# One gated recurrence and a two-branch layer on one core: block 0's layers taken by quarters of the weights, and the input casts and transposing DMAs run as a pipeline of single tensors, three items ahead

## The chip, the core and the metric

The kernel runs on one core of a Trainium2 chip. Its engines work side by side, each through its own queue in program order, and they wait for one another by semaphores: TensorE (PE in the profile; its weight loads are listed as PEld), VectorE (DVE), ScalarE (ACT), GpSimd (POOL) and SyncE (SP), which here only issues DMAs. Sixteen DMA engines serve all DMA queues of the core. The metric is the device time of one execution in microseconds. Time before: 400.93 us, the median of 6 runs (400.65 to 401.17).

## The reference

The input `x` and `f_logit` are 4 x 6144 x 256 in fp32, `lower_bound` has 256 entries. The first part is a recurrence over time, one for each batch row and channel; the second is a layer with two branches, of which the larger is kept:

```python
sig = 1 / (1 + exp(-f_logit))
f = lower_bound + (1 - lower_bound) * sig
for t in range(S):                       # S = 6144
    h = f[:, t] * h + (1 - f[:, t]) * x[:, t]
    y[:, t] = h
h1 = y @ w1;  h2 = y @ w2                # 256 -> 1024
out = max(h1, h2) @ w_out                # 1024 -> 256
```

## The kernel before, in words

**The algebra.** With u = sigmoid(-f_logit) and om = 1 - lower_bound, 1 - f is om * u. The kernel scans y' = ff * y' + u * x with ff = 1 - om * u, so that the true y is om * y'; the factor om is put into the weights. max(h1, h2) is h1 + relu(h2 - h1), so it makes `wd` = om * (w2 - w1) in bf16, and `w13` = om * (w1 @ w_out), which needs w1 transposed (`w1T`). The output is relu(y' @ wd) @ w_out + y' @ w13.

**The tiles.** Time is cut into 48 blocks of 512 steps (`TB`), 12 for each batch row. Channels lie on the partitions, in two halves (`KC` = 2). For a block, `hidden(j, fc)` makes one of eight chunks of 128 hidden units: two matmuls of 512 columns into a PSUM tile `dT`, then a relu into `rt` (ScalarE, or VectorE where `on_dve`). `project_steps(j, i, lo, hi)` makes a quarter i of the block's tokens out of eight `rt` chunks and two steps with `w13`: ten matmuls of 256 columns into `psO`. A block thus has 16 hidden and 40 projecting matmuls. `store` copies a PSUM tile to SBUF and issues the DMA to the output from SP.

**The input.** The natural layout has time on the rows, so it must be transposed. Blocks 0 to 2 are loaded in fp32 (`load`), turned to u and v in natural layout (`gate_nat`, `drive_nat`), and transposed by TensorE (`turn_pe`); then come `forget` (ff) and `scan`. From block 3 on, POOL issues DMAs that copy `f_logit` and `x` to DRAM scratch with a cast to bf16 (`cast`, tiles `fs` and `xs`), and SP issues transposing DMAs from there into SBUF (`turn_dma`, tiles `fT` and `xT`); `gate`, `drive`, `forget` and `scan` then work in the transposed layout. Before, an item of this chain is a chunk of two blocks (`CB` = 2; the first has one), both tensors together, with two sets of scratch (`NS`). POOL holds the next cast back by a one-column copy (`held`) out of the transposed tile before it (`cast_after_turn`).

**The order.** Everything runs under `tc.manual_schedule()`: the program order below is each engine's order. Loads first (L397 to L416): they alternate blocks of `x`, `f_logit` and quarters of w1 and w2, and w_out in two halves. Then block 0 and the making of the weights are woven together by hand (L421 to L517): `diff` (w2 - w1) on POOL, the last quarter on VectorE; `scale` (times om) on ScalarE; `turn_w1` transposes w1 in fp32 on TensorE, `keep_w1` copies it out; `linear_weights` makes w13's sums in two halves. `keep_warm` issues matmuls on zeros. The main loop (L525) does for block j and chunk fc: hidden(j, fc), a half-slot of projection of block j - 1, and, at places given by the tables `gate_at` and `turn_of` (L378 to L384), the gate and scan of a block two ahead and the transposing DMAs of a chunk three ahead. Block 1's projection is done in the loop pass j = 2.

Of the kernel before, what the change touches and what calls it, by code (L numbers as in the profile page):

```python
# [12 lines left out]
P = 128  # L13
# [3 lines left out]
def kernel(  # L17
# [25 lines left out]
    NP = 3  # L43
    CB = 2
    assert NBB % CB == 0
    chunks = [(NP, 1)] + [(j, CB) for j in range(NP + 1, NBLK, CB)]
    NCH = len(chunks)
    home = {j + o: (c, o) for c, (j, n) in enumerate(chunks) for o in range(n)}
    NS = 2
# [8 lines left out]
    ttpool = ctx.enter_context(tc.tile_pool(name="turned", bufs=3))  # L58
# [3 lines left out]
    opool = ctx.enter_context(tc.tile_pool(name="opool", bufs=4))  # L62
# [11 lines left out]
    w1n = wpool.tile([P, KC, DFF], FP32)  # L74
    w2n = wpool.tile([P, KC, DFF], FP32)
# [63 lines left out]
    def scan(j, h, t0=0, t1=TB):  # L139
# [18 lines left out]
    rows, chunk = {}, {}  # L158

    spare = {  # L160
        (k, name): scratch.tile([CB * TB, D], BF16, name=f"{name}{k}")
# [4 lines left out]
    def cast(c):  # L166
        j, n = chunks[c]
        b, k = divmod(j, NBB)
        rows[c] = []
        for name, src in (("fs", f_logit), ("xs", x)):  # L170
            t = spare[c % NS, name]
            nc.gpsimd.dma_start(  # L172
                out=t[0 : n * TB, :],
                in_=src[b, k * TB : (k + n) * TB, :],
                max_dma_last_dim=4096,
            )
            rows[c].append(t)

    def turn_dma(c):
        n = chunks[c][1] * TB  # L180
        for s in range(2):
            t = ttpool.tile([P, KC, CB * TB], BF16, name=("fT", "xT")[s])
            chunk[c, s] = t
            nc.sync.dma_start_transpose(out=t[:, :, 0:n], in_=rows[c][s][0:n, :])

    def gate(j):
        c, o = home[j]
        us[j] = midpool.tile([P, KC, TB], BF16, name="u")
        nc.scalar.activation(  # L189
            out=us[j][:],  # L190
            in_=chunk[c, 0][:, :, o * TB : (o + 1) * TB],
            func=AF.Sigmoid,
            scale=-1.0,
        )
        uT[j] = us[j]

    def drive(j):
        c, o = home[j]
        vT[j] = midpool.tile([P, KC, TB], BF16, name="v")
        nc.vector.tensor_tensor(  # L200
            out=vT[j][:],
            in0=us[j][:],
            in1=chunk[c, 1][:, :, o * TB : (o + 1) * TB],
            op=ALU.mult,
        )
# [67 lines left out]
    def store(j, g):  # L273
        osb = opool.tile([P, 2, D], FP32, name="osb")
        nc.vector.tensor_copy(out=osb[:], in_=pos[j, g, 0][:])  # L275
        r0 = j * TB + 2 * g * P
        nc.sync.dma_start(
            out=out[r0 : r0 + 2 * P, :].rearrange("(p r) d -> p r d", r=2), in_=osb[:]
        )

    def store_row(j, g, r):
        osb = opool.tile([P, 2, D], FP32, name="osb")
        ps = pos[j, g, r]
        nc.vector.tensor_copy(out=osb[:, 0, 0:P], in_=ps[:, 0, 0:P])
        nc.scalar.copy(out=osb[:, 0, P:D], in_=ps[:, 0, P:D])
# [3 lines left out]
            in_=osb[:, 0, :],  # L289
# [5 lines left out]
    def weight_load(k, w, src):  # L295
        cols = slice(k * QF, (k + 1) * QF)
# [4 lines left out]
    def wout_load(g):  # L301
        nc.sync.dma_start(
            out=won[:, 4 * g : 4 * g + 4, :],
            in_=moe_w_out[g * HF : (g + 1) * HF, :].rearrange("(q p) c -> p q c", p=P),
# [20 lines left out]
    def scale(k, h):  # L325
        cols = slice(k * QF, (k + 1) * QF)
        nc.scalar.activation(
            out=wd[:, h, cols], in_=wdf[:, h, cols], func=AF.Copy, scale=om[:, h : h + 1]
        )

    pts = {}

    def turn_w1(k):
        pts[k] = ps_d.tile([P, 2, D], FP32, name="dT")
        for q in range(2):
            for h in range(KC):
                nc.tensor.transpose(
                    pts[k][:, q, h * P : (h + 1) * P],
                    w1n[:, h, unit(2 * k + q)],
                    ident[:],  # L340
                )

    def keep_w1(k):
        nc.scalar.copy(out=w1T[:, 2 * k : 2 * k + 2, :], in_=pts[k][:])
# [33 lines left out]
    gate_at = {NP: (1, 7), NP + 1: (3, 2), NP + 2: (3, 6), NP + 3: (5, 0), NP + 4: (5, 5)}  # L378
    gate_at |= {b: (b - 2, 5) for b in range(NP + 5, NBLK)}
    gate_of = {}  # L380
    for b, at in gate_at.items():
        gate_of.setdefault(at, []).append(b)
    turn_of = {(1, 3): 1}
    turn_of |= {(chunks[c][0] - 3, 5): c for c in range(2, NCH)}  # L384

    def cast_after_turn(c):

        last = chunks[c - 1][1] * TB - 1
        nc.gpsimd.tensor_copy(out=held[:], in_=chunk[c - 1, 0][:, KC - 1, last : last + 1])  # L389
        cast(c)  # L390

    with tc.manual_schedule():
# [4 lines left out]
        nc.scalar.dma_start(out=lbr[:], in_=lower_bound.rearrange("(h p) -> h p", p=P))  # L397
        load(0, 0, 0, 2)
        load(0, 1, 0, 2, nc.scalar)
        for k in range(2):  # L400
            weight_load(k, w1n, moe_w1)
            weight_load(k, w2n, moe_w2)
            if k == 0:
                load(0, 0, 2, 4)
                load(0, 1, 2, 4)
        wout_load(0)
        for k in range(2, 4):
            weight_load(k, w1n, moe_w1)
            weight_load(k, w2n, moe_w2)
        for s in range(2):  # L410
            load(1, s, 0, 2)
        wout_load(1)
# [8 lines left out]
        keep_warm(6)  # L421
        keeps()
        keep_warm(2)


        gate_nat(0, 0, 2)
        drive_nat(0, 0, 2)
        for s in range(2):
            for q in range(2):
                turn_pe(0, s, q)  # L430
        forget(0, 0, 0, HB, on_act=True)
        forget(0, 1, 0, HB)
        for h in range(KC):
            scan(0, h, 0, HB)
        diff(0, 0, KC, nc.gpsimd)
        turn_w1(0)
        keep_warm(3)
        gate_nat(0, 2, 4)
        drive_nat(0, 2, 4)
        for s in range(2):  # L440
            for q in range(2, 4):
                turn_pe(0, s, q)
        scale(0, 0)
        forget(0, 0, HB, TB, on_act=True)
        forget(0, 1, HB, TB)
        scale(0, 1)
        keep_w1(0)
        for fc in range(2):
            hidden_cols(0, fc, 0, HB)
        for h in range(KC):  # L450
            diff(1, h, h + 1, nc.gpsimd)
        for h in range(KC):
            scan(0, h, HB, TB)
        turn_w1(1)
        for h in range(KC):
            scale(1, h)
        nc.gpsimd.tensor_copy(out=wob[:, 0:4, :], in_=won[:, 0:4, :])
        for fc in range(2):
            hidden_cols(0, fc, HB, TB)
            relu(0, fc, on_dve=(fc == 1))  # L460
        for fc in range(2, 4):
            hidden(0, fc, on_dve=(fc == 3))
        keep_w1(1)
        for h in range(KC):
            diff(2, h, h + 1, nc.gpsimd)
        for h in range(KC):
            scale(2, h)
        for s in range(2):
            for i in range(4):
                project_steps(0, i, s, s + 1)  # L470
        turn_w1(2)
        for s in range(2, 4):
            for i in range(4):
                project_steps(0, i, s, s + 1)
        keep_w1(2)
        diff(3, 0, KC, nc.vector)
        for h in range(KC):
            scale(3, h)
        for fc in range(4, 6):
            hidden(0, fc, on_dve=(fc == 5))  # L480
        linear_weights(0, 4)
        turn_w1(3)
        gate_nat(1, 0, 2)
        drive_nat(1, 0, 2)
        keep_w1(3)


        for q in range(2):
            turn_pe(1, 0, q)
        for h in range(KC):  # L490
            forget(1, h, 0, HB, on_act=True)
        for fc in range(6, 8):
            hidden(0, fc, on_dve=(fc == 7))
        nc.gpsimd.tensor_copy(out=wob[:, 4:8, :], in_=won[:, 4:8, :])
        for q in range(2):
            turn_pe(1, 1, q)
        for h in range(KC):
            scan(1, h, 0, HB)
        gate_nat(1, 2, 4)
        drive_nat(1, 2, 4)  # L500
        linear_weights(4, 8)
        keep_linear()
        for s in (4, 5, 6):
            for i in range(4):
                project_steps(0, i, s, s + 1)
        for q in range(2, 4):
            turn_pe(1, 0, q)
        forget(1, 0, HB, TB, on_act=True)
        forget(1, 1, HB, TB)
        for i in range(4):  # L510
            project_steps(0, i, 7, 8)
# [4 lines left out]
        for i in range(4):  # L516
            project_steps(0, i, 8, 10)  # L517


        nc.gpsimd.tensor_copy(out=held[:], in_=ins[2][0][:, NQ - 1, D - 1 : D])  # L520
        cast(0)
        turn_dma(0)
        cast_after_turn(1)

        for j in range(1, NBLK + 1):  # L525
            if j == 2:
                for slot in range(4):
                    project(1, slot)
            for fc in range(FC):
                if j < NBLK:  # L530
                    hidden(j, fc, on_dve=(j == 1 and fc % 2 == 1))
# [5 lines left out]
                if j == 1:  # L537
                    if fc == 0:
                        gate_nat(2, 0, NQ)
                        drive_nat(2, 0, NQ)  # L540
                        store(0, 0)
                    if fc == 3:
                        store(0, 1)
                    if fc in (5, 6):
# [57 lines left out]
```

## Time and profile before

| what | value |
|---|---|
| median of 6 runs | 400.93 us |
| profiled execution | 401.9 us, of which span 400.1 us |
| TensorE busy (matmul) | 385.8 us, 96% of the span |
| ScalarE, VectorE, GpSimd busy | 271.6, 248.8, 46.1 us |
| granted TensorE clock | 1.00 in the whole span |
| DMA | 79.13 MB, mean 198 GB/s |
| casting DMAs of f_logit and x (two blocks each) | 22 + 22, 512 KB written each; 1 + 1 of one block |
| transposing DMAs | 23 + 23 |

The profiled execution is one run, 1.0 us over the median. In the profile, busy time counts what an engine's instructions took; a wait of an engine is put down to the last semaphore that came. A row of the timeline gives start, busy time, engine, line, operation, output <- inputs, shape and count, and in square brackets the idle time before it with its releaser.

### The profile page before, as it was taken

The page shows a single profiled execution, that of the slowest core. Times are in us where ns is not written, and L with a number is a line of the kernel's source. Part 1 is how long each engine was busy: PE and PEld are TensorE (multiplying, and loading weights), DVE is VectorE, ACT ScalarE, POOL GpSimd, SP SyncE. Part 2 cuts the span into 40 slices and gives each one's busy share as a digit, 9 for nine tenths or more (in the row PEclk, how much of TensorE's full clock was granted, in tenths as well). Part 3 has the DMA queues.
Part 4 walks back from the last instruction along what each step waited for, and adds up shares of the span by engine and source line. Part 5 has one row for each costly group of instructions (what it writes and reads, how often), then busy time and mean ns, then how long its engine had stood idle before and what let it go on. Part 6 is the DMA issues. An engine that isn't in the chain of part 4 may idle for free.

```text
span 400.1 us, 7192 instructions
## 1 busy us (share of the span) xinstructions
PE 385.8 (96%) x2736; PEld 270.2 (68%) x2784; DVE 248.8 (62%) x353; ACT 271.6 (68%) x450; POOL 46.1 (12%) x82
## 2 busy tenths in 40 slices
PE   6989899999999999999999999999999999999996
PEld 3656577667776677667766777677766776677664
DVE  4577548676576567657656765775576567657621
ACT  4856667766766676676667667766766776676661
POOL 2420110011012020120210110110101101100000
PEclk9999999999999999999999999999999999999999
DMA  8979999999999999899999999998989999996122
GB/s 258 349 156 176 205 209 251 223 216 203 216 196 213 209 179 241 183 179 233 194 183 222 196 197 209 194 230 186 199 218 187 187 221 204 184 220 145 54 102 84
DMA packets 126359, 79.13 MB, mean 198 GB/s; under 512 B 96242, under 2 KB 102644, under 8 KB 126324
## 3 DMA queue, kind: packets, MB, share of 16 engines
q1 hardware_dynamic: 113792, 54.80, 54.7%
q0 software_dynamic: 12256, 23.60, 36.5%
q8 instruction: 22, 0.36, 0.4%
q10 hardware_dynamic: 276, 0.26, 0.2%
q14 instruction: 13, 0.11, 0.1%
HBM read 53.48 MB, written 48.76 MB: 256 GB/s over the span
## 4 chain that ended last, share of the span: by engine, by line
PE 86%; DMA 10%; DVE 1%; issue 1%; POOL 0%; ACTq 0%; SPq 0%; ACT 0%; DVEq 0%; POOLq 0%
PE psO L259 49%; PE dT L221 37%; DMA xs<-in_x_dram 2%; DMA fn<-in_f_logit_dram 2%; DMA w2n<-in_moe_w_dram 2%; DMA xT<-xs 1%; DMA xn<-in_x_dram 1%; DMA fT<-fs 1%; DMA fs<-in_f_logit_dram 1%; DVE y L148 1%; DVE v L200 0%; POOL held L520 0%; POOL fs L172 0%; ACTq L397 0%; DVE ff L135 0%
## 5 line engine op out<-in xcount | busy, mean ns | idle before, releaser
L236 ACT ACTIVATE rt<-dT 128x512 bf16<-128x512 f32 x376 | 219.0, 596 | 113.3 <-PE dT L221 113.0
L259 PE MATMUL psO<-wob,rt 128*128 128x256 bf16 x1536 | 228.9, 273 | 0.3 <-DVE rt L234 0.2
L221 PE MATMUL dT<-y,wd 128*128 128x512 bf16 (+1 forms) x724 | 217.3, 378 | 6.5 <-DVE y L148 2.4
L259 PEld LDWEIGHTS <-rt 128*128 128x128 bf16 x1536 | 150.2, 98 | 97.3 <-issue 1.5
L148 DVE TENSOR_TENSOR_SCAN y<-ff,y,v 128x512 bf16<-128x512 bf16 x84 | 107.8, 1283 | 3.0
L200 DVE TENSOR_TENSOR v<-u,xT 128x1024 bf16<-128x1024 bf16 x45 | 31.1, 691 | 101.8 <-ACT u L189 91.7
L221 PEld LDWEIGHTS <-wd 128*128 128x128 bf16 x772 | 75.1, 98 | 15.6 <-issue 3.6
L275 DVE COPY osb<-psO 128x512 f32<-128x512 f32 x95 | 64.2, 678 | 29.0 <-PE psO L259 29.0
L259 PE MATMUL psO<-w,y 128*128 128x256 bf16 x384 | 72.8, 273 | 0.0
L189 ACT ACTIVATE u<-fT 128x1024 bf16<-128x1024 bf16 x45 | 47.2, 1049 | 0.1
L389 POOL CAST held<-fT 128x1 f32<-128x1 bf16 x22 | 13.7, 623 | 287.9 <-DMA fT<-fs 287.9
L259 PEld LDWEIGHTS <-y 128*128 128x128 bf16 x384 | 37.5, 98 | 4.3
L135 DVE TENSOR_SCALAR ff<-u,nom 128x512 bf16<-128x512 bf16 x90 | 30.4, 338 | 0.0
L172 POOL DMA_DIRECT2D fs<-in_f_logit_dram x23 | 12.8, 556 | 2.0 <-issue 1.8
L172 POOL DMA_DIRECT2D xs<-in_x_dram x23 | 12.6, 548 | 0.0
L148 DVE TENSOR_TENSOR_SCAN y<-ff,v 128x512 bf16<-128x512 bf16 x6 | 7.4, 1225 | 0.2
L234 DVE TENSOR_SCALAR rt<-dT 128x512 bf16<-128x512 f32 x8 | 5.3, 685 | 2.4 <-PE dT L221 2.4
L148 DVE TENSOR_TENSOR_SCAN y<-ff,y,dT 128x256 bf16<-128x256 bf16 (+1 forms) x8 | 6.6, 863 | 0.1
L110 DVE TENSOR_TENSOR vn<-un,xn 128x512 bf16<-128x512 bf16 (+1 forms) x5 | 3.9, 789 | 4.3 <-ACT un L103 2.7
L370 PE MATMUL psO<-warm 128*128 128x512 bf16 x11 | 4.3, 529 | 1.2 <-DVE warm L418 1.2
L103 ACT ACTIVATE un<-fn 128x512 bf16<-128x512 f32 (+1 forms) x5 | 3.6, 713 | 2.4 <-DMA fn<-in_f_logit_dram 2.4
L318 POOL TENSOR_TENSOR wdf<-w2n,w1n 128x256 f32<-128x256 f32 (+1 forms) x5 | 4.1, 836 | 7.7 <-DMA w2n<-in_moe_w_dram 7.7
(34 smaller groups left out, 37.9 us busy)
## 6 DMA issues: line engine op xcount, KB each, us to landing
out_dram<-osb SPq DMA_DIRECT2D x95, 256.0 KB, 3.1
fs<-in_f_logit_dram POOLq DMA_DIRECT2D x22, 512.0 KB, 5.9
xs<-in_x_dram POOLq DMA_DIRECT2D x22, 512.0 KB, 9.2
fn<-in_f_logit_dram SPq DMA_DIRECT2D x4, 256.0 KB, 5.9
w1n<-in_moe_w_dram SPq DMA_DIRECT2D x4, 256.0 KB, 5.8
w2n<-in_moe_w_dram SPq DMA_DIRECT2D x4, 256.0 KB, 6.4
won<-in_moe_w_out_dram SPq DMA_DIRECT2D x2, 512.0 KB, 6.5
xn<-in_x_dram SPq DMA_DIRECT2D x3, 256.0 KB, 6.8
```

Source lines behind the costliest of these rows:

```text
L135: nc.vector.tensor_scalar(out=o, in0=i, scalar1=nom[:, h : h + 1], scalar2=1.0, op0=ALU.mult, op1=ALU.add)
L148: nc.vector.tensor_tensor_scan(out=ys[j][:, h, t0:t1], data0=ffs[j][:, h, t0:t1], data1=vT[j][:, h, t0:t1], initial=initial, op0=ALU.mult, ...
L172: nc.gpsimd.dma_start(out=t[0 : n * TB, :], in_=src[b, k * TB : (k + n) * TB, :], max_dma_last_dim=4096,)
L189: nc.scalar.activation(out=us[j][:], in_=chunk[c, 0][:, :, o * TB : (o + 1) * TB], func=AF.Sigmoid, scale=-1.0,)
L200: nc.vector.tensor_tensor(out=vT[j][:], in0=us[j][:], in1=chunk[c, 1][:, :, o * TB : (o + 1) * TB], op=ALU.mult,)
L221: nc.tensor.matmul(dts[j, fc][:, t0:t1], lhsT=wd[:, kc, unit(fc)], rhs=ys[j][:, kc, t0:t1], start=(t0 == 0 and kc == 0), stop=(t1 == TB an ...
L234: nc.vector.tensor_relu(out=rt[:], in_=dts[j, fc][:])
L236: nc.scalar.activation(out=rt[:], in_=dts[j, fc][:], func=AF.Relu)
L259: nc.tensor.matmul(ps, lhsT=lhsT, rhs=rhs, start=(s == 0 and (r == 0 or alone)), stop=(s == FC + KC - 1 and (r == 1 or alone)), skip_group ...
L275: nc.vector.tensor_copy(out=osb[:], in_=pos[j, g, 0][:])
L370: nc.tensor.matmul(idle[:].rearrange("p r d -> p (r d)"), lhsT=warm[:, 0:P], rhs=warm[:], start=True, stop=True,)
L389: nc.gpsimd.tensor_copy(out=held[:], in_=chunk[c - 1, 0][:, KC - 1, last : last + 1])
```

## The change

Neither the computation nor its types at the borders change. Three things do.

*Loads and block 0.* The loads of block 0 come first, half of the ScalarE queue's and half of SP's; then, quarter by quarter, w1, w2 and w_out. Block 0's inputs are gated, transposed and scanned whole before the first layer; then a loop over the four weight quarters does: two hidden chunks, `prepare` of the next quarter (w1 rounded to bf16 on POOL, w2 - w1 on POOL or, for the last, VectorE, the scaling one half on ScalarE and one on VectorE, w_out rounded on POOL), the transposes of w1 in bf16, two sums of the linear weights, and the projection of the two chunks.

*Blocks 1 and 2.* The gate of block 2 stands ahead of block 1's layers; its transposes, and half of the projection of block 1, are woven into block 1's layers. The two output tiles of block 0 are copied by ScalarE at the end of block 1.

*Input chain.* An item is one tensor of one block. Three casts are issued at the start; when an item is transposed, POOL issues the cast of the item three ahead. Scratch has three sets, transposed tiles five buffers, output tiles six. The tables say for each block where its transposes and its gate stand. The last two output rows are copied by VectorE alone.

```diff
-    ttpool = ctx.enter_context(tc.tile_pool(name="turned", bufs=3))
+    ttpool = ctx.enter_context(tc.tile_pool(name="turned", bufs=5))
-    opool = ctx.enter_context(tc.tile_pool(name="opool", bufs=4))
+    opool = ctx.enter_context(tc.tile_pool(name="opool", bufs=6))
...
-    def cast(c):
...
+    def cast(j, s):
         b, k = divmod(j, NBB)
-        for name, src in (("fs", f_logit), ("xs", x)):
-            t = spare[c % NS, name]
-            nc.gpsimd.dma_start(out=t[0 : n * TB, :], ...)
+        nc.gpsimd.dma_start(
+            out=spare[j % NS, ("fs", "xs")[s]][:],
+            in_=(f_logit, x)[s][b, k * TB : (k + 1) * TB, :],
+            max_dma_last_dim=4096,
+        )
+    def turn_dma(j):
+        for s, name in enumerate(("fs", "xs")):
+            t = ttpool.tile([P, KC, TB], BF16, name=("fT", "xT")[s])
+            turned[j, s] = t
+            nc.sync.dma_start_transpose(out=t[:], in_=spare[j % NS, name][:])
         for s in range(2):
...
+            b, k = divmod(2 * j + s + 3, 2)
+            if b < NBLK:
+                nc.gpsimd.tensor_copy(
+                    out=held[:], in_=turned[j, s][:, KC - 1, TB - 1 : TB]
+                )
+                cast(b, k)
...
-        nc.vector.tensor_copy(out=osb[:, 0, 0:P], in_=ps[:, 0, 0:P])
-        nc.scalar.copy(out=osb[:, 0, P:D], in_=ps[:, 0, P:D])
+        nc.vector.tensor_copy(out=osb[:], in_=pos[j, g, r][:, 0, :])
...
-    gate_at = {NP: (1, 7), NP + 1: (3, 2), NP + 2: (3, 6), NP + 3: (5, 0), NP + 4: (5, 5)}
-    gate_at |= {b: (b - 2, 5) for b in range(NP + 5, NBLK)}
...
-    turn_of = {(1, 3): 1}
-    turn_of |= {(chunks[c][0] - 3, 5): c for c in range(2, NCH)}
+    turn_of, gate_of = {}, {(1, 7): [NP], (2, 7): [NP + 1]}
+    for b in range(NP + 2, NBLK):
+        at = max(FC * 3 + 7 * (b - NP - 2), FC * (b - 3) + 3)
+        turn_of[divmod(at, FC)] = b
+        gate_of.setdefault(divmod(max(at + 6, FC * (b - 2) + 4), FC), []).append(b)
...
+        def prepare(k, on_dve):
+            round_w1(k)
+            if on_dve:
+                diff(k, 0, KC, nc.vector)
+            else:
+                for h in range(KC):
+                    diff(k, h, h + 1, nc.gpsimd)
+            scale(k, 0)
+            scale(k, 1, on_dve=True)
+            round_wout(k)
+
+        prepare(0, False)
+        turn_w1(0)
+        keep_w1(0)
+        keep_warm(4)
+        for k in range(4):
+            for fc in (2 * k, 2 * k + 1):
+                hidden(0, fc, on_dve=(fc % 2 == 1))
+            if k == 2:
+                gate_nat(1, 0, 2)
+                drive_nat(1, 0, 2)
+            if k < 3:
+                prepare(k + 1, k == 2)
+            if k == 2:
+                for q in range(2):
+                    turn_pe(1, 0, q)
+                for h in range(KC):
+                    forget(1, h, 0, HB, on_act=True)
+            if k < 3:
+                turn_w1(k + 1)
+                keep_w1(k + 1, on_dve=(k + 1 == 3))
+            linear_weights(2 * k, 2 * k + 2)
...
+            for s in (2 * k, 2 * k + 1):
+                for i in range(4):
+                    project_steps(0, i, s, s + 1)
...
+        gate_nat(2, 0, NQ)
+        drive_nat(2, 0, NQ)
-        nc.gpsimd.tensor_copy(out=held[:], in_=ins[2][0][:, NQ - 1, D - 1 : D])
-        cast(0)
-        turn_dma(0)
-        cast_after_turn(1)
+        nc.gpsimd.tensor_copy(out=held[:], in_=ins[1][1][:, NQ - 1, D - 1 : D])
+        for i in range(3):
+            cast(*divmod(2 * NP + i, 2))
+        turn_dma(NP)
+        turn_dma(NP + 1)
 
         for j in range(1, NBLK + 1):
-            if j == 2:
-                for slot in range(4):
-                    project(1, slot)
             for fc in range(FC):
...
                 if j == 1:
-                    if fc == 0:
-                        gate_nat(2, 0, NQ)
-                        drive_nat(2, 0, NQ)
-                        store(0, 0)
...
+                    if fc >= 2:
+                        for i in range(2):
+                            project_steps(1, i, fc - 2, fc - 1)
+                    if fc == 7:
+                        for g in range(2):
+                            store(0, g, on_act=True)
+                        for i in range(2):
+                            project_steps(1, i, 6, 10)
```

## The prediction

> **What bounds the kernel now.** I read the page's busy shares and its chain first, then busy time by stage, then the rows of TensorE where it stood still, last the DMA chain that feeds it.
>
> ```profile
> PE 385.8 (96%) x2736; PEld 270.2 (68%) x2784; DVE 248.8 (62%) x353; ACT 271.6 (68%) x450; POOL 46.1 (12%) x82
> ...
> PE 86%; DMA 10%; DVE 1%; issue 1%; POOL 0%; ACTq 0%; SPq 0%; ACT 0%; DVEq 0%; POOLq 0%
> ```
>
> TensorE is the bound, and a DMA holds the chain only at its start. The stages say where TensorE stands still (columns: length, then busy time and count of PE, PEld, DVE, ACT, POOL, then clock, DMA share, GB/s):
>
> ```profile
> 5.00:23.50 18.50, 15.11 (x125) 10.85 (x126) 12.21 (x20) 12.39 (x26) 8.47 (x10) 1.00 0.99 305
> 23.50:50.00 26.50, 22.90 (x156) 14.71 (x160) 18.09 (x25) 17.31 (x28) 2.55 (x6) 1.00 1.03 188
> 50.00:100.00 50.00, 49.69 (x353) 35.06 (x359) 33.20 (x47) 34.84 (x57) 5.31 (x12) 1.00 1.09 220
> 100.00:350.00 250.00, 248.32 (x1760) 175.19 (x1791) 161.02 (x224) 176.07 (x288) 29.09 (x48) 1.00 0.97 202
> ```
>
> From 50 us on nothing can be won: projecting steps start every 0.9775 us (54.05, 55.03, 56.01 and 56.98 in the chain), and from 49.33 to 391.45 there are 342.1 / 0.9775 = 350.0 of them, without a gap. All that the change can move lies before 50 us and in the last 4 us. These rows are block 1's first layer and TensorE's stops after it:
>
> ```profile
> 23.49 2.53 PE L221 MATMUL dT<-y,wd 128*128 128x512 bf16 x10 [0.26 <-DVE y L148]
> 27.95 0.59 PE L221 MATMUL dT<-y,wd 128*128 128x512 bf16 x2 [1.36 <-DVE rt L234]
> 32.70 0.81 PE L221 MATMUL dT<-y,wd 128*128 128x512 bf16 x2 [0.55 <-DVE y L148]
> 47.81 0.38 PE L221 MATMUL dT<-y,wd 128*128 128x512 bf16 x1 [1.17 <-DVE y L148]
> ```
>
> So I use three marks: A, the second matmul of block 1 (23.49); B, the second matmul of block 4 (47.81); and the last matmul's end (396.20). The work between A and B is 48 hidden matmuls of 0.2175, 80 projecting ones of 0.1087 and 16 transposes of 0.055, 20.0 us; it took 24.32, so 4.3 us were lost. B to the end is 348.4 us with no loss. The other rows that the sum uses:
>
> ```profile
> 9.68 1.41 POOL L318 TENSOR_TENSOR wdf<-w2n,w1n 128x256 f32<-128x256 f32 x2 [1.64 <-DMA w2n<-in_moe_w_dram]
> 11.18 1.04 POOL L457 CAST wob<-won 128x1024 bf16<-128x1024 f32 x1
> 17.20 1.43 POOL L494 CAST wob<-won 128x1024 bf16<-128x1024 f32 x1 [3.01 <-DMA won<-in_moe_w_out_dram]
> 24.62 1.34 SPq L184 DMA_TRANSPOSE fT<-fs  x1
> 28.80 0.19 POOL L389 CAST held<-fT 128x1 f32<-128x1 bf16 x1 [6.67 <-DMA fT<-fs]
> 43.92 0.69 DVE L200 TENSOR_TENSOR v<-u,xT 128x1024 bf16<-128x1024 bf16 x1 [4.90 <-DMA xT<-xs]
> ```
>
> POOL does little in block 0 now (two differences 1.41, a cast of 1024 columns 1.04 alone and 1.43 beside VectorE's product). A transposing DMA of one block lands about 4.1 us after its issue. The product of block 4 waits 4.9 us for its tensor: that is the loss ahead of B.
>
> **The change, part by part.** The profiled execution took 401.9 us: its span of 400.1 and 1.8 around it. It is 1.0 above the median of 400.93; differences from the span are added to the median.
>
> *1. Loads and block 0, up to A.* The first w1 quarter moves from second to fifth place on the loading queues, w2's to sixth. In the trace the fifth and sixth loads land at 7.36 and 8.17 (issue 2.26 + 5.1, 2.77 + 5.4). POOL gets two casts of 512 columns per quarter: half of 1.04 to 1.43, so 0.52 to 0.72, I take 0.62. Its chain: w1 cast 7.4 to 8.0, differences from 8.2 to 9.6, w_out cast to 10.2; second quarter 0.62 + 1.41 + 0.62, to 12.9; third quarter's differences end at 14.9. Block 0's scans end near 10.3 (10.85 now), so POOL sets the pace, not they. Then, in order: scaling on VectorE 0.35 (nearest row: a 128x256 scale-and-add, 0.34), to 15.3; hidden chunk 4 and its relu (0.60), to 16.6; the gate of block 1 behind it on ScalarE (0.63), to 17.2. From there VectorE is the chain: product 0.69, last difference 0.69, scaling 0.35, copy of w1T about 0.65, two half scans 1.39, relu 0.69, with about 0.08 of overlap each: 21.55. Then four projecting matmuls, four transposes, a ScalarE step 0.47 and two half scans 1.39: A at 24.7 against 23.49, +1.2. The bf16 transposes of w1 (four take 0.60 in fp32 now, 0.39 in bf16) and the more keep-warm matmuls lie in TensorE's waits for POOL: 0. Bounds: A at 24.0 if casts take 0.52 and the loads bind (the twelfth load lands at 12.67, plus 1.41 for the differences: 14.1 in place of 14.9); at 26.0 if POOL and VectorE hold each other up at every meeting. The one such meeting in the trace cost 1.43 - 1.04 = 0.39, so I add 0.4: **+1.6** (+0.5 to +2.5).
>
> The Trainium skill, SBUF — State Buffer, section "SBUF: two separate sides", speaks against this part: GpSimd and a VectorE instruction that uses both ports share a port pair, and whoever holds it makes the other wait its whole length. POOL would go on to its w_out cast just before VectorE starts the new scaling, which would so wait some 0.55 us in each of three quarters, the last of them on the path. By that rule alone the term would be an estimated +1.8; no row of this trace shows VectorE held by POOL.
>
> *2. A to B.* The 1.36 came from relu (1,1) queueing on VectorE behind block 2's product (1.23) and a store's copy (0.68); the product now precedes block 1's layers, the copies go to ScalarE at block 1's end, and half of block 1's projection fills the gaps. What is late next is a relu on VectorE (about 0.3) and block 1's last relu on ScalarE, wanted by projection at once (about 0.45). The wait for xT of block 4 (4.9 us on VectorE, 1.5 on TensorE) goes: the casts start when block 1's last part of x lands (18.7, by issue 11.90 + 6.8) rather than block 2's logits (20.2), and each tensor is cast and transposed alone; casts from 19.0, fT of block 3 at 19.0 + 3.7 + 4.1 = 26.8, the cast of x of block 4 behind it to 31.9, its xT by 36 to 37, and its gate runs at 37.7. Lost now 4.3, then 0.7: **-3.6** (-4.1 to -2.5).
>
> *3. A new wait behind B.* Block 5's transposes stand in pass 3 behind the store of block 1's second half on SP, and that store's copy stands on VectorE behind block 4's scans. With t the start of block 3 on TensorE: gate 4 starts at t + 0.2 on ScalarE, product to second scan's end takes 1.1 + 3.84 (43.92 to 47.76 now), so t + 5.2; copy 0.68, store issue 0.5: the transposing DMA is issued at t + 6.35 and lands 4.06 later (24.62 to 28.68), t + 10.4. Gate 5 waits for it on ScalarE in front of the relu of chunk (3,7): 1.05 + 0.60 and hand-overs, t + 12.3. TensorE wants that chunk in block 4's second half-slot, t + 7.82 + 1.63: 2.9. The store issued 0.5 us ahead puts 256 KB on the same DMA engines, 0.75 us at the 350 GB/s of the loads, of which I add 0.15: **+3.05**; block 4's relus queue behind too, but they have t + 8 to t + 10 and five PSUM tiles. Bounds by the landings of all such DMAs, 3.6 to 6.6: +2.4 to +5.4. I take the one-block row, the only one of that size with its tensor ready.
>
> *4. The steady state.* An item's round is the held copy 0.2 to 1.1, the cast's issue 0.55, landing 3.7 and 4.3 (one block), transposing 3.6 to 4.1: 8.1 to 10. Three in flight at two per block may take 3 x 7.82 / 2 = 11.7: **0**. From the rows of two-block items (6.4, 4.9) it would be 13.0, 1.3 too long per 1.5 blocks, some +37 in all: the far end. POOL's 65 more small copies and twice as many DMA issues hide behind its idle 88%. SP's issues are 45 + 45 in place of 23 + 23, at 1.2 to 1.3 us for one block: SP spends its time waiting for stores' copies (211 us), which covers them; were it gone, stores would be late, with six output tiles as cover.
>
> *5. The tail.* Last copies now 396.24 to 396.83 (VectorE 0.29, then ScalarE 0.27); one copy of 256 columns lies between 0.29 and 0.68, 0.42 by the line between: **-0.2**.
>
> Sum: 1.6 - 3.6 + 3.05 + 0 - 0.2 = +0.85: 401.8 us.
>
> **The rivals.** *Block 0 as fast as now* (faster): the early transposes and halved scaling pay, and the 0.55 us by which block 0's scans end earlier reach A, 22.9; then -0.6 - 3.6 + 3.05 - 0.2 = -1.35, 399.6. It decides at A below 23.4 (400.1). For it: those scans. Against it: POOL's 2.6 us per quarter.
> *The new wait is long*: stores and casts on the same DMA engines (share 0.97 to 1.09) stretch that transposing DMA to 5.5 to 6.6 us, or ports hold up block 0 fully: 403 to 404.5. For it: two-block landings up to 6.6; against: few DMAs are in flight then.
> *The pipeline does not keep pace*, so that the change doesn't do what it says: ScalarE's gates wait for fT in every block or third block, 406 (0.1 us in each of 43 blocks and the 0.85) to 438. It decides at a round above 11.7 us. Against it: the DMA engines' total work is the same.
>
> **How the numbers follow.** Told from no change is what exceeds 0.2%, 0.8 us. My forecast, 400.7 to 402.8, has 0.60: some 0.31 of it within 0.8 us of 400.93 and 0.29 above. The faster rival 0.15 (0.13 under 400.13, 0.02 within); the long wait 0.17; lost pace 0.08. Faster 0.13, same 0.33, slower 0.54. The range runs from 400.2 (A at 23.9, landing 3.6: 0.4 - 3.6 + 2.6 - 0.2 = -0.8) to 404.3, the long wait's upper part; the forecast's own is 400.7 to 402.8.
>
> **What would show it.** A between 24.4 and 25.4; no stop over 0.6 between A and B; one stop of TensorE of 2.4 to 3.5 us in block 4, projection waiting for a ScalarE relu, and gate u waiting for fT ahead of it; 0.9775 per step after. Wrong if A is under 23.4, if block 4 runs through, or if stops recur.

## The result, and the profile after

The changed kernel took 405.77 us (median of 35 runs, 401.22 to 411.63) against 401.16 (median of 70 runs, 400.56 to 404.66): a ratio of 1.0083, 95% interval 1.0069 to 1.0098, so slower by about 1%. The ratio, here and below, leaves out runs more than 1.5% above the kernel's fastest (nine of these 35) and is therefore below the quotient of the medians, 1.0115; as the spread turns out to be the kernel's own, the medians say more. The forecast was 401.8 with a range up to 404.3; the time lies above the range, just below the low edge of the rival "the pipeline does not keep pace" (406).

The times themselves are the first finding: 4.1 us lie between the fastest and the slowest of the 70 runs of before (0.5 in the six that the prediction had), and 10.4 us between those of the changed kernel. The granted clock does not explain the spread: the twelve runs of the changed kernel whose mean clock was 1.000 took from 401.22 to 411.63 us, the whole range. The profiled execution, 403.0 us with a span of 401.1, is one of the faster ones. Its busy shares and its chain by engine:

```profile
PE 386.7 (96%) x2737; PEld 269.0 (67%) x2786; DVE 247.0 (62%) x352; ACT 270.4 (67%) x449; POOL 88.5 (22%) x198
...
PE 88%; DMA 4%; ACT 2%; DVE 2%; issue 1%; POOL 1%; SPq 1%; ACTq 0%; DVEq 0%
```

TensorE is still the bound, but in the chain the DMAs' 10% have become 4%, half of it `fT<-fs`, and ScalarE and VectorE have 2% each (0% and 1% before). The stages (columns as before: length, then busy time and count of PE, PEld, DVE, ACT, POOL, clock, DMA share, GB/s):

```profile
5.00:23.50 18.50, 15.57 (x128) 9.86 (x131) 12.79 (x23) 11.35 (x25) 11.39 (x18) 1.00 1.08 320
23.50:50.00 26.50, 23.67 (x165) 15.43 (x167) 17.90 (x24) 19.07 (x32) 4.67 (x12) 1.00 0.85 169
50.00:100.00 50.00, 49.69 (x353) 34.88 (x358) 32.59 (x47) 34.40 (x58) 12.04 (x25) 1.00 1.11 195
100.00:350.00 250.00, 247.03 (x1745) 173.66 (x1776) 158.95 (x224) 174.30 (x287) 55.58 (x127) 1.00 1.12 202
```

The fourth row holds what is new: between 100 and 350 us TensorE was busy 247.03, against 248.32, where the prediction had put nothing. (Some matmul records are missing from both traces: the row of before is 1.68 short of 250 though its steps follow one another without a gap. The difference of the two rows, 1.29, is real.) The DMA share went from 0.97 to 1.12 there, with the same bytes. TensorE's rows at the marks and at its stops:

```profile
24.16 0.38 PE L218 MATMUL dT<-y,wd 128*128 128x512 bf16 x1 [0.46 <-DVE y L145]
24.80 0.38 PE L218 MATMUL dT<-y,wd 128*128 128x512 bf16 x1 [0.26 <-DVE y L145]
30.87 0.28 PE L256 MATMUL psO<-wob,rt 128*128 128x256 bf16 x1 [0.27 <-ACT rt L233]
48.57 0.28 PE L256 MATMUL psO<-wob,rt 128*128 128x256 bf16 x1 [1.68 <-ACT rt L233]
```

A is the second row, 24.80. Between A and block 4 there is one stop of 0.27. Block 4 has the one stop that was forecast, 1.68; ahead of it stand block 5's transposing DMA on SP and the gate that waits for it:

```profile
43.51 1.30 SPq L176 DMA_TRANSPOSE fT<-fs  x1
46.98 1.06 ACT L187 ACTIVATE u<-fT 128x1024 bf16<-128x1024 bf16 x1 [2.54 <-DMA fT<-fs]
```

The page of waits (us in all, times, longest) shows the rest:

```profile
POOL held L180 <- DMA fT<-fs: 171.0, 43, 10.0
...
DVE v L197 <- DMA xT<-xs: 62.2, 23, 5.3
...
ACT u L187 <- DMA fT<-fs: 18.1, 14, 3.3
```

Fourteen of 45 gates waited for their transposing DMA, and 23 products for theirs (before: 2 products, 7.6 us in all). One round of the input chain, from the timeline:

```profile
184.18 0.71 POOL L180 CAST held<-xT 128x1 f32<-128x1 bf16 x1 [5.20 <-DMA xT<-xs]
184.83 0.52 POOL L165 DMA_DIRECT2D fs<-in_f_logit_dram  x1
190.59 1.23 SPq L176 DMA_TRANSPOSE fT<-fs  x1
...
196.69 1.06 ACT L187 ACTIVATE u<-fT 128x1024 bf16<-128x1024 bf16 x1 [3.28 <-DMA fT<-fs]
198.28 0.28 PE L256 MATMUL psO<-wob,rt 128*128 128x256 bf16 x1 [0.69 <-ACT rt L233]
```

An xT lands at 184.1, POOL makes its small copy and issues the cast of the item three ahead. Its transposing DMA goes out at 190.59 and lands at 196.6, 12.5 us after the landing that began the round. The gate had waited 3.28 us, and TensorE stops behind it. Stops that recur were named in the prediction as a sign of its being wrong.

The time between the profiled executions (403.0 - 401.9 = +1.1) comes out in these parts. A is 1.31 later. From A to the end of the last matmul 372.87 us passed, against 372.71. Without any loss it is 20.0 + 348.4 = 368.4, so 4.47 were lost in place of 4.31: 0.5 up to the second matmul of block 4 (4.3 before), 1.85 for block 4's stop and what hangs on it, and 2.1 in the steady state, nearly all of it between 188 and 200 us. Behind the last matmul 3.47 us passed, against 3.92. A median run took 2.8 us more than the profiled one.

### The profile page after: what moved, and what is told of

It is laid out like the page before. It is cut to its first block, busy times and chain, and to the rows that moved or that the text cites. A ratio compares the mean times of both kernels' runs of the same rounds, so it can differ in the third digit from the quotient of the medians.

```text
span 401.1 us, 7472 instructions
## 1 busy us (share of the span) xinstructions
PE 386.7 (96%) x2737; PEld 269.0 (67%) x2786; DVE 247.0 (62%) x352; ACT 270.4 (67%) x449; POOL 88.5 (22%) x198
## 4 chain that ended last, share of the span: by engine, by line
PE 88%; DMA 4%; ACT 2%; DVE 2%; issue 1%; POOL 1%; SPq 1%; ACTq 0%; DVEq 0%
PE psO L256 51%; PE dT L218 36%; DMA fT<-fs 2%; DMA w2n<-in_moe_w_dram 1%; ACT rt L233 1%; DVE y L145 1%; ACT u L187 1%; POOL wdf L321 1%; DVE osb L275 0%; PE dT L119 0%; DVE wdf L321 0%; ACT ff L128 0%; SPq L90 0%; DVE v L197 0%; POOL w1b L344 0%
## 5 line engine op out<-in xcount | busy, mean ns | idle before, releaser
L233 ACT ACTIVATE rt<-dT 128x512 bf16<-128x512 f32 x377 | 216.5, 596 | 97.0 <-PE dT L218 96.3
L218 PE MATMUL dT<-y,wd 128*128 128x512 bf16 x719 | 217.3, 379 | 1.7 <-DVE y L145 0.7
L275 DVE COPY osb<-psO 128x512 f32<-128x512 f32 x93 | 60.6, 676 | 27.2 <-PE psO L256 27.0
L187 ACT ACTIVATE u<-fT 128x1024 bf16<-128x1024 bf16 x45 | 47.3, 1052 | 18.4 <-DMA fT<-fs 18.1
L180 POOL CAST held<-fT 128x1 f32<-128x1 bf16 x44 | 10.4, 236 | 171.0 <-DMA fT<-fs 171.0
L180 POOL CAST held<-xT 128x1 f32<-128x1 bf16 x43 | 23.2, 539 | 86.7 <-DMA xT<-xs 86.5
L165 POOL DMA_DIRECT2D xs<-in_x_dram x45 | 23.2, 515 | 10.1 <-issue 9.6
L165 POOL DMA_DIRECT2D fs<-in_f_logit_dram x45 | 23.4, 520 | 2.7 <-issue 2.5
L387 PE MATMUL psO<-warm 128*128 128x512 bf16 x17 | 6.0, 483 | 1.2 <-DVE warm L424 1.2
L128 ACT ACTIVATE ff<-dT,nom 128x256 bf16<-128x256 bf16 (+1 forms) x10 | 4.6, 512 | 1.7 <-PE dT L119 1.7
```

Source lines behind the costliest of these rows:

```text
L165: nc.gpsimd.dma_start(out=spare[j % NS, ("fs", "xs")[s]][:], in_=(f_logit, x)[s][b, k * TB : (k + 1) * TB, :], max_dma_last_dim=4096,)
L180: nc.gpsimd.tensor_copy(out=held[:], in_=turned[j, s][:, KC - 1, TB - 1 : TB])
L187: nc.scalar.activation(out=us[j][:], in_=turned[j, 0][:], func=AF.Sigmoid, scale=-1.0,)
L218: nc.tensor.matmul(dts[j, fc][:, t0:t1], lhsT=wd[:, kc, unit(fc)], rhs=ys[j][:, kc, t0:t1], start=(t0 == 0 and kc == 0), stop=(t1 == TB an ...
L233: nc.scalar.activation(out=rt[:], in_=dts[j, fc][:], func=AF.Relu)
L387: nc.tensor.matmul(idle[:].rearrange("p r d -> p (r d)"), lhsT=warm[:, 0:P], rhs=warm[:], start=True, stop=True,)
```

## The experiments

Theory 1: the ring of three items (copy, cast, transposing DMA, and the copy again) has no spare time. Rivals: the DMA engines are full whatever is in flight (theory 2), or twice as many DMAs and copies cost a fixed amount (theory 3). Times stand against the kernel before on the same chip in the same hour (medians 400.9, 401.35, 401.06 and 401.49 in the four groups of runs).

### The length of the ring

*Two items ahead.*

```diff
-            b, k = divmod(2 * j + s + 3, 2)
+            b, k = divmod(2 * j + s + 2, 2)
...
-        for i in range(3):
+        for i in range(2):
             cast(*divmod(2 * NP + i, 2))
```

> The changed kernel with its casts two items ahead in place of three. Theory 1 (the ring of three items is too short: cast, transposing DMA, small POOL copy and the next cast follow each other, and a round of 11.7 us on average in the trace meets the 11.7 us that three items allow): two items allow 7.82 us, the round falls with fewer transfers in flight but not below about 8.5 us (shortest landings in the trace 4.0 for a cast and 3.2 to 3.4 for a transposing DMA, plus the copy, the issue and the hand-overs), so each of 43 blocks takes 8.5 to 10 us: 435 to 500 us. Theory 2 (the DMA engines are full, however many items are in flight): two items keep them as busy as three, 404 to 408. Theory 3 (a fixed cost of twice as many DMAs and small copies): 404 to 408.

Measured: 456.77 us, ratio 1.1394 (1.1362 to 1.1427). That is 55.9 more than before over 43 blocks, 1.30 each, so a round took about 9.1 us. Theories 2 and 3 fall: neither the work of the DMA engines nor the number of DMAs and copies changed, and the time rose by 56 us. The waits of the gates, 43 in all:

```profile
ACT u L187 <- DMA fT<-fs: 114.7, 43, 4.5
```

*Six items ahead* (the same edit, with 6 in the place of 3).

> The changed kernel with its casts six items ahead in place of three, nothing else. Theory 1 (ring too short): six items allow 23.5 us for a round, so a late landing is made up, no stop of TensorE is left in the steady state, the wait in block 4 stays: 399.8 to 401.2, with a spread as small as that of the kernel before. Theory 2 (DMA engines full): the landings grow with what is in flight, to 8 us and more, the stops stay, 404 or more. Theory 3 (fixed cost of twice as many DMAs and copies): 404 to 407 as it is.

Measured: 401.46 (400.88 to 402.43), ratio 1.0016 (1.0006 to 1.0026). Theory 1 holds: the spread is 1.5 us over twelve runs in place of 10, and TensorE stands still nowhere from 100 to 350 us (this trace lacks no matmul records there, so 250.00 is not to be set against the 248.32 of before).

```profile
100.00:350.00 250.00, 250.00 (x1792) 175.14 (x1790) 160.76 (x225) 175.92 (x288) 50.44 (x130) 1.00 1.12 204
```

Block 4's stop stayed, and with it the time, 0.26 above the range I gave:

```profile
48.70 0.28 PE L256 MATMUL psO<-wob,rt 128*128 128x256 bf16 x1 [1.51 <-ACT rt L233]
```

The landings did grow, as theory 2 said, but not to the 8 us that it expected, and the steady state had no stop. The pages' DMA issues (KB each, median us from issue to landing) with two, three and six items in flight, in this order:

```profile
fs<-in_f_logit_dram POOLq DMA_DIRECT2D x45, 256.0 KB, 4.6
xs<-in_x_dram POOLq DMA_DIRECT2D x45, 256.0 KB, 4.9
fT<-fs SPq DMA_TRANSPOSE x45, 3.5
xT<-xs SPq DMA_TRANSPOSE x45, 3.2
```

```profile
fs<-in_f_logit_dram POOLq DMA_DIRECT2D x45, 256.0 KB, 5.3
xs<-in_x_dram POOLq DMA_DIRECT2D x45, 256.0 KB, 5.4
fT<-fs SPq DMA_TRANSPOSE x45, 5.6
xT<-xs SPq DMA_TRANSPOSE x45, 4.4
```

```profile
fs<-in_f_logit_dram POOLq DMA_DIRECT2D x45, 256.0 KB, 5.0
xs<-in_x_dram POOLq DMA_DIRECT2D x45, 256.0 KB, 6.4
fT<-fs SPq DMA_TRANSPOSE x45, 6.5
xT<-xs SPq DMA_TRANSPOSE x45, 6.6
```

From the issue and landing times of the single items between 100 and 350 us I worked out the mean round, in us. A ring that keeps up takes as long for a round as its depth allows, so the spare time shows in the column "waiting for SP":

| in flight | copy and issue | cast | waiting for SP | transposing DMA | round | allowed |
|---|---|---|---|---|---|---|
| 2 | 0.65 | 4.79 | 0.12 | 3.53 | 9.1 | 7.8 |
| 3 (the changed kernel) | 0.64 | 5.59 | 0.37 | 5.22 | 11.8 | 11.7 |
| 4 (with block 5 earlier, below) | 0.61 | 5.81 | 2.47 | 6.66 | 15.5 | 15.6 |
| 6 | 0.62 | 5.66 | 10.33 | 6.56 | 23.2 | 23.5 |

With three items the work of a round is 0.64 + 5.59 + 5.22 = 11.45 us of the 11.7 allowed. One landing of 10 us (the longest were 10.2 and 11.1) is some 4.5 above the mean, and at 0.3 of spare time per round it takes many rounds to make up. That the number of such landings makes the times differ from run to run is not shown, since only one run has a trace. With four, 2.5 us per round are spare.

*Half of the stores left out* (those of the first half of blocks 5 to 45; the copies out of PSUM stay).

```diff
         r0 = j * TB + 2 * g * P
+        if g == 0 and 5 <= j < NBLK - 2:
+            return
```

> The changed kernel without the stores of the first half of blocks 5 to 45 (their copies out of PSUM stay; this part of the output is left out). The stores carry 256 KB each and take a third to a fifth of the DMA time. If what stretches the landings of casts and transposing DMAs is the stores beside them: their medians fall from 5.3 and 5.6 to about 4.8 and 4.6, the round to 10 to 10.5 us, and the stops in the steady state go: 400 to 402. If casts and transposing DMAs stretch each other and the stores matter little: landings within 0.3 us of now, 403.5 to 406.

Measured: 402.11 (400.90 to 403.64), ratio 1.0029 (1.0014 to 1.0043); no stop between 50 and 350 us in its trace (block 4's, 2.10 us at 49.0, is there). The landings were 5.2 and 4.7 for the casts, 5.4 and 4.4 for the transposing DMAs, so only the cast of x changed by more than 0.2. Neither expectation fits whole: the stops went, but the work of a round fell only from 11.45 to 11.29. (For 11 of the 90 transposing DMAs this trace has no landing.) The run agrees with a ring that stands near its limit. How much of the stretching is due to the stores' bytes and how much to their place on SP it does not separate.

### Block 5's place on SP

*Its transposing DMAs one slot earlier, three items ahead.*

```diff
-        turn_of[divmod(at, FC)] = b
+        turn_of[divmod(at - (b == NP + 2), FC)] = b
```

> The changed kernel with block 5's transposing DMAs one slot earlier, ahead of the store of block 1's second half on SP; three items ahead stay. If the stop of 1.7 us in block 4 comes from that store standing ahead of the DMA: fT of block 5 is issued near 36 in place of 43.5, the stop is gone, and the time falls by about 1.85 against the changed kernel, 403 to 404.5, while the steady state's stops stay. If that stop comes from the cast or the landing instead: no stop goes, 405 to 406.5. If the ring's losses all start with this late item: 400.5 to 401.5.

Measured: 402.71 (399.85 to 410.36), ratio 1.0029 (1.0001 to 1.0057). SP's rows show the DMA at 37.64, behind the store of block 1's first half, in place of 43.51:

```profile
37.22 0.33 SPq L277 DMA_DIRECT2D out_dram<-osb  x1
37.64 1.51 SPq L176 DMA_TRANSPOSE fT<-fs  x1
39.25 2.11 SPq L176 DMA_TRANSPOSE xT<-xs  x1
```

The tensor lands at 42.4 and the gate runs without a wait; the stop in block 4 is gone, and others remain (1.06 at 79.0). So the DMA's place on SP, behind the store of block 1's second half, was the cause. Against the kernel before, the medians went from +4.6 to +1.8: a gain of 2.8, above the 1.85 of the stop, so that the time lies between the expectations. The next items start earlier too, but three of twelve runs are still above 405, so the late item was not where all the losses began.

*The same with six items ahead.*

> Six items ahead, and block 5's transposing DMAs one slot earlier, ahead of the store of block 1's second half; the changed kernel's loads and block 0. With six items ahead alone the trace had one stop of 1.51 us at 48.70, projection waiting for a ScalarE relu behind the gate of block 5. If that stop comes from the store ahead of the DMA, it goes, and nothing else stops TensorE by more than 0.3 us after A: 401.5 - 1.5 - up to 0.8 lost in blocks 4 to 9 behind it = 399.2 to 400.2. If six items crowd block 5's transfers, so that they land no earlier: 401 to 402.

Measured: 399.77 (398.94 to 400.79), ratio 0.9962 (0.9946 to 0.9978): faster than before. After A (25.49 here) the largest stop is 0.27.

*The same with four.*

> The changed kernel with four items ahead and block 5's DMAs one slot earlier: between the runs with three (402.71) and six (399.77), which are otherwise the same. The work of a round (copy, cast, transposing DMA, without waits for SP) was 11.3 to 11.45 us with three in flight, against 11.7 allowed; with four it was 13.6 in the run with the old start, against 15.6. If the ring's spare time is what counts, four is as good as six: 399.2 to 400.2, spread under 2.5 us. If more depth only thins out the late transfers: about halfway, 400.8 to 401.8.

Measured: 399.39 (398.63 to 399.58), ratio 0.9939 (0.9917 to 0.9961). Four are as good as six.

### The parts of the change alone

*The new loads, block 0 and block 1, with the chain of the kernel before.*

```diff
-        for i in range(3):
-            cast(*divmod(2 * NP + i, 2))
-        turn_dma(NP)
-        turn_dma(NP + 1)
+        cast(0)
+        turn_dma(0)
+        cast_after_turn(1)
```

(cast, turn_dma, gate, drive, the tables, two sets of scratch and three turned tiles as before the change.)

> The changed kernel's loads, block 0, block 1 and tail, with the casts and transposing DMAs of the kernel before (two blocks at a time, two chunks), started from the new place. If the new order of block 1 earned most of the 3.6 us between A and B: A at 24.8, at most 1.2 us of the wait for xT of block 4 left, no stop after 50 us: 399 to 400.3, with a small spread. If the pipeline of single tensors earned it: a stop of 2 us or more before B, 401 to 402.5. If the losses of the changed kernel after 50 us do not come from its chain: 404 or more.

Measured: 399.19 (398.81 to 399.44), ratio 0.9941 (0.9921 to 0.9960). From A (25.29) to the last matmul's end it took 368.98 us, 0.6 above the 368.4 without loss. So the new order of block 1, with the first cast at 18.68 in place of 20.91, which this run keeps, earned all that term 2 had put down to it and to the single tensors, and the slowdown sits in the chain of single tensors.

*The old loads and block 0, six items ahead, block 5 earlier.*

```diff
-        for k in range(4):
-            if k == 3:
-                for s in range(2):
-                    load(1, s, 0, 2)
-            weight_load(k, w1n, moe_w1)
-            weight_load(k, w2n, moe_w2)
-            wout_load(k)
...
+        wout_load(0)
+        for k in range(2, 4):
+            weight_load(k, w1n, moe_w1)
+            weight_load(k, w2n, moe_w2)
```

> As the run with six items ahead and block 5's DMAs one slot earlier, but with the loads and block 0 of the kernel before: w_out in halves, w1 transposed in fp32, all scalings on ScalarE. If the weight quarters cost the 1.3 us by which A came later (24.80 against 23.49): 1.0 to 1.4 below that run, 398 to 399. If the later A was already covered, or the new order of block 1 needs the new block 0 to run without stops: within 0.4 of that run, 399.2 to 400.2, with A at 23.5 and new stops of about 1 us between A and B.

Measured: 400.67 (399.08 to 405.19), ratio 0.9985 (0.9959 to 1.0011): not faster than with the new start, and above both expectations. A was at 23.15, 2.3 earlier than there, and TensorE stood still 3.80 us at 49.1; this traced run took 403.01, 2.3 above the median, so its stop may be longer than the usual one. SP issued block 5's DMA at 36.91 and it landed 10.5 later (6.6 in the run with the new start), among six items' transfers.

*The old loads and block 0, with the old chain.*

> The new order of block 1 and 2, the copies of block 0 on ScalarE and the new tail, with the loads, block 0 and the two-block chain of the kernel before: the change without its weight quarters and without its single tensors. With the new start and the old chain the kernel took 399.19, and A lay between 24.8 and 25.5 in the traces with the new start, 23.2 to 23.5 with the old one. If the quarters cost what A shows and the order of block 1 does not need them: 397.0 to 398.0, with a spread under 1 us. If the order needs the new block 0: stops of 1 us or more between A and B, 398.4 to 399.5.

Measured: 400.32 (399.45 to 402.39), ratio 0.9983 (0.9968 to 0.9999): above both expectations. The product of block 4, first with the new start and old chain, then with the old start:

```profile
41.99 0.69 DVE L201 TENSOR_TENSOR v<-u,xT 128x1024 bf16<-128x1024 bf16 x1 [3.33 <-ACT u L190]
```

```profile
41.40 0.69 DVE L201 TENSOR_TENSOR v<-u,xT 128x1024 bf16<-128x1024 bf16 x1 [4.46 <-DMA xT<-xs]
```

With the old start A is at 23.57, 1.7 earlier, but the product can start only 0.6 earlier: it waits for a DMA whose chain begins when block 1's x has landed, at 18.4 and 18.7. TensorE then stops 1.04 us at 45.30. Over the traces A lay at 24.46 to 25.49 with the new start (mean of eight 24.98) and at 23.15 to 23.57 with the old one (mean of five 23.33), so the new loads and block 0 cost 1.65 at A. That this lead reaches the end needs inputs that come earlier too.

*All scalings on ScalarE* (new start, old chain).

```diff
-            scale(k, 1, on_dve=True)
+            scale(k, 1)
```

> The new start with the old chain, with the second half of each quarter's scaling back on ScalarE. In the changed kernel's trace VectorE's scaling takes 0.67 us where POOL's w_out cast runs beside it, and 0.33 to 0.35 where it does not. If POOL and VectorE holding each other up is what makes the new block 0 slower: the scalings then take 0.51 each on ScalarE and hold nothing up, A comes 0.3 to 1 us earlier than in the run with VectorE, 398.2 to 398.9. If POOL's chain of two casts and two differences sets the pace: A within 0.3, 398.9 to 399.5. If ScalarE is the one that is full there: A later by up to 0.9 (the last two quarters' 0.51, less overlap), 399.5 to 400.1.

Measured: 399.16 (398.81 to 400.40), ratio 0.9951 (0.9933 to 0.9969), against 399.19. A was at 24.84, 0.45 earlier, in one trace each, within what the new start spreads by; the time did not move. The meetings of POOL and VectorE in the changed kernel's block 0 look like this:

```profile
10.05 0.33 DVE L332 TENSOR_SCALAR wd<-wdf,om 128x256 bf16<-128x256 f32 x1
...
12.16 0.60 POOL L306 CAST wob<-won 128x512 bf16<-128x512 f32 x1
12.25 0.67 DVE L332 TENSOR_SCALAR wd<-wdf,om 128x256 bf16<-128x256 f32 x1 [0.27 <-POOL wdf L321]
...
17.11 0.69 DVE L107 TENSOR_TENSOR vn<-un,xn 128x512 bf16<-128x512 bf16 x1
17.17 1.10 POOL L306 CAST wob<-won 128x512 bf16<-128x512 f32 x1 [0.88 <-DMA won<-in_moe_w_out_dram]
17.71 1.10 DVE L321 TENSOR_TENSOR wdf<-w2n,w1n 128x512 f32<-128x512 f32 x1
```

The scaling beside POOL's cast took 0.67 in place of 0.33, and ended 0.16 after it. The cast and the difference took 1.10 each in place of 0.60 and 0.69. The lock in the Trainium skill's page "SBUF — State Buffer", section "SBUF: two separate sides", leads one to expect such waits, but longer ones: after a wait for the cast's whole length the scaling would have ended 0.33 behind it, not 0.16, and the delay was 0.33 where the prediction had worked out 0.55 per quarter. The unchanged time fits the expectation that POOL's casts and differences set the pace of the quarters; A's 0.45 fits the other, so this run does not settle it.

### Both cures together

*The old loads and block 0, four items ahead, block 5 earlier.*

> As the run with the old loads and block 0, with four items ahead in place of six. Four items allow 15.6 us for a round, against 11.7 on average and at most 17.1 in the changed kernel's trace. If one item more than the average needs is enough: the same as with six within 0.4 us, 398 to 399.2, the landings shorter by about 0.5 us since less is in flight. If the rare late transfers (10 to 11 us) need more cover: 0.5 to 2 us above six, with a wider spread.

Measured: 398.70 (397.35 to 402.50), ratio 0.9937 (0.9913 to 0.9961). The median lies in the range given, but 2.0 below the run with six, not within 0.4 of it. The landings were not shorter than with six (the work of a round was 13.6 us, against 13.4, as the sum of the means of those landings that the two traces have; 22 of the 90 transposing DMAs lack theirs in each), and two of twelve times lie above 401.

*Four items ahead, the old start, and the transposing DMAs of blocks 5 to 9 at the place of the steady state.*

```diff
-        turn_of[divmod(at, FC)] = b
+        turn_of[divmod(FC * (b - 3) + 3, FC)] = b
```

> Four items ahead with the loads and block 0 of the kernel before, and the transposing DMAs of blocks 5 to 9 at the place that the steady state gives them (block 5's at the fourth slot of block 2, ahead of both stores of block 1), gates unchanged. In the run with four items fT of block 5 landed at 44.1, when ScalarE had waited for it 1.3 us, and two of twelve times were 3 us above the others. If its late place on SP is the cause: landed by 43.4, no stop, 397.2 to 398.4, without times above 400. If SP now stands waiting for the casts of block 5 with the stores behind it: 398.6 to 400.5.

Measured: 398.33 (396.95 to 399.25), ratio 0.9920 (0.9891 to 0.9948): the lowest median of all, ahead of both kernels. Its traced fT of block 5 landed at 43.2 and no stop above 0.27 is left:

```profile
50.00:100.00 50.00, 50.00 (x361) 35.06 (x359) 33.34 (x47) 35.42 (x59) 11.95 (x27) 1.00 1.19 223
100.00:350.00 250.00, 250.00 (x1792) 175.13 (x1791) 160.82 (x225) 175.87 (x288) 50.50 (x129) 1.00 1.13 202
```

In the traces its last matmul ends at 392.07, against 393.38 for four items with the new start and 396.20 before (the first two are the fastest runs of their kernels). By the times alone the two starts are not told apart (0.9920 and 0.9939, with overlapping intervals).

## Why the prediction was wrong

*Term 1, loads and block 0 (+1.6).* Right in size. A at 24.80 lies in the 24.4 to 25.4 given; over the traces the cost is 1.65. The third quarter's differences end at 14.78 (14.9 forecast), and POOL and VectorE hold each other up by 0.41 at the last difference, the 0.4 added. The rival of a fast block 0 is out. But the sum does not close as written: from 17.2 the listed pieces of VectorE, with the overlap given, reach about 21.2, not 21.55, and from there to A they come to 2.5 where 3.15 was taken (the trace: 3.09, from 21.71). So nearly 1 us had no stated source, and part of the hit is luck.

*Term 2, A to B (-3.6).* Right in size: 4.3 lost before, 0.5 now, so -3.8. Wrong in one cause: with the new start, the early first cast and the two-block chain the same gain appears, so the single tensors were not needed for it. Part of it hangs on the later A: with the old start and the two-block chain 1.7 us were lost between A and B (23.57 to 45.30), 1.04 of them in the stop there.

*Term 3, the wait behind B (+3.05).* The mechanism was right and the size off: 1.85. The issue was placed at t + 6.35, which with block 3's start near 37.3 is 43.65, and came at 43.51. The landing took 3.4 in place of 4.06, the gate, the relu and their hand-overs about 0.2 less than put down, TensorE wanted the chunk some 0.15 later, and the 0.15 added for the store's bytes did not show.

*Term 4, the steady state (0).* This is the step that failed. It took the landings of block 3's transfers, 3.7 and 4.3 for a cast and 3.6 to 4.1 for a transposing DMA, made when the DMA share was low (0.74 and 0.83 in the stretches of 20 to 25 and 25 to 30 us, against 0.97 from 100 to 350), and came to a round of 8.1 to 10 us. With three items in flight they take 5.59 and 5.22 on the mean, and the round is 11.8 where 11.7 are allowed. The step's own far end, 13.0 from the two-block rows, was nearer to the truth than the value taken. (Its 6.4 was misread: it is the median of the casts of x and the transposing DMAs that read them, taken together; the casts alone have medians of 5.9 and 9.2.) The argument against the rival, that the DMA engines' work is the same, was true and beside the point: the ring is bound by how long each transfer takes, not by how much there is to move. At 0.08 the rival was priced far too low for a margin of which one side of the sum was unmeasured. The traced run lost 2.1 us there; if the further 2.8 us of a median run lie there too, as the small spread with four and six items suggests but no trace shows, it lost 4.9.

*Term 5, the tail (-0.2).* -0.45 in the two traces.

Sum in the profiled execution, by the marks: 1.31 - 3.8 + 1.85 + 2.1 - 0.45 = +1.0, against +1.1 measured. That this is near the forecast +0.85 is luck: term 3 was 1.2 too large and term 4 was 2.1 too small. (The low end of the range, -0.8, is 400.1, not 400.2.) The medians differ by 4.6: the changed kernel's lies 2.8 above its profiled run, that of before 0.7 below its own.

## What to carry to other kernels

Where a chain of dependent transfers runs a fixed number of items ahead, work out its round from landings measured with that many in flight, not from the first transfers of a run; if the round comes within a few per cent of what the depth allows (11.45 of 11.7 here), expect a wide spread of times and add one item. An item more cost nothing here (399.39 with four, 402.71 with three), and scratch for it was there already. A stage that ends earlier is worth only as much as the next input's arrival lets through: with the two-block chain, 1.7 us of lead at A became a stop of 1.04 in block 4.

## What the hardware showed unexpectedly

A transposing DMA of the same 512 rows took 3.2 to 3.5 us to land (medians) with two items in flight, 4.4 to 5.6 with three and 6.5 to 6.6 with six, while the casts' medians went from 4.6 and 4.9 only to 5.0 and 6.4. Its issue grows with it, and holds up what stands behind it on SP's queue. SP's rows with six items in flight, where the same issue takes 1.23 us when little is in flight:

```profile
93.22 5.07 SPq L176 DMA_TRANSPOSE xT<-xs  x1
98.39 1.18 SPq L277 DMA_DIRECT2D out_dram<-osb  x2
```

The rare landings of about 10 us and more (9.8 at 160.7 and 11.1 at 341.7 in the changed kernel's trace) came in stretches where the casts beside them were long too, 7.4 to 10.2, while a store issued at 341.2 landed in 4.0. What starts such a stretch these runs do not show.
